# An attention and MoE kernel on one core: loads, splits, turns and swaps moved to other slots, stores a slot later, three buffers for turned k and q, one k turned on TensorE

## The chip, the cores and the metric

The kernel runs on one core of a Trainium2 chip. The metric is the time of one execution on the device in microseconds. Three runs of the kernel before gave 509.38, 513.93 and 518.40 us; the time before is their median, 513.93 us. A profile of one further execution is given below.

A core has a matrix engine (TensorE, PE in the profile; its weight loads are PEld), a vector engine (VectorE, DVE), a scalar engine (ScalarE, ACT), a general engine (GpSimd, POOL), and a sync engine (SyncE, SP). SP and ACT also issue DMA transfers, each from its own instruction queue (SPq and ACTq). An engine takes its instructions in program order.

## The reference

q, k and v are 8 batches of 8 heads, 576 rows of 64 numbers, in float32. The attention drops scores that are more than `tau` under their row's maximum; its output goes through two matrix products with `h - tanh(h)` between them.

```python
scores = scale * np.matmul(q, k.transpose(0, 1, 3, 2))
thresh = np.max(scores, axis=-1, keepdims=True) - tau
scores = np.where(scores >= thresh, scores, -1000000000.0)
scores = scores - np.max(scores, axis=-1, keepdims=True)
attn = np.exp(scores)
attn = attn / (np.sum(attn, axis=-1, keepdims=True) + 1e-09)
attn_out = np.matmul(attn, v)
# heads side by side: x is 4608 x 512
h = x @ w_in                      # 512 x 2048
out = (h - np.tanh(h)) @ w_out    # 2048 x 512
```

## The kernel before

**Tiles and slots.** Two heads make a pair, and there are 32 pairs, four to a batch. A pair has nine tiles of 128 score rows (`TPP = 9`), 288 tiles in all. The main loop (from L820) runs over slots, one tile to a slot: in slot `s` the scores of tile `s + 8` are computed (`AHEAD = 8`), the thresholded exponent of tile `s + 5` is begun (`kink`, L425, writes z), and tile `s` is weighted with v (`weights`, L442, and `attend`, L474). Between these the loop drops steps of the two MoE products of the batch four pairs back: `hidden` (L561, one step is four matmuls) and `project` (L589, likewise), in a pattern of 36 slots. After the 288 slots the MoE work that is left over runs alone.

**q and k.** The scores need q and k with more than half precision, so each is split into a high and a low float16 part. Each pair goes through a chain: load, split, turn, swap.

- Load: pairs 0 to 7 by SP (`load`, L174). From pair 8 on (`DUAL = 8`) by ACT's queue (`load_part`, L143), in five transfers: one for k, two for q, two for v. They fill `raw` buffers, two for each of k, q and v.
- Split: `split` (L222), three POOL instructions that write `khl` or `qhl` (two buffers each); `split_v` (L255), three POOL instructions.
- Turn: `turn` (L297) brings the head dimension onto the partitions. Up to pair 7 TensorE transposes nine 128x128 chunks into PSUM (L281) and DVE copies the result out (L313). From pair 8 on one DMA transpose issued by SP does it (L301). The results `kT` and `qT` are in a pool of two buffers.
- Swap: `swap` (L318), two POOL copies of 64x1152 (L323), which exchange the halves of kT into `kS`, also two buffers. Scores are the sum of q against kT and q against kS.

**z.** From pair 6 on, z of two tiles at a time is transposed by a DMA transpose issued by SP (L440) into `zT`; ACT takes the exponent of that (L469) as pT, the weights of `attend`. In pairs 0 to 5 TensorE does this transpose (L452, L461).

**What sets the order.** Nothing is scheduled automatically. For the chain of each pair there is a table of distances: an entry `("kt", 7)` in `LATER` puts the turn of k seven slots before the slot in which the pair's first scores are computed. Pairs 8 and up use one table for even and one for odd pairs; pairs 1 to 7 use `PREP` (L733) with exceptions. All steps of a slot's plan come at its end. In the tables k0 is the load of k, q0 and q1, v0 and v1 the two parts of the others, ks, qs and vs the splits, kt and qt the turns, kw the swap. SP's queue thus holds, in the order of the slots: the z transposes (in even slots), the turns of k and q, the output stores (L606), and in the beginning loads of q, k, v and the MoE weights. A store is collected in `stores` by `project` and issued in the next slot with the exception of the last one collected (L852 to L854), which waits for a later one.

Of the kernel before, what the change touches and what calls it, by code (L numbers as in the profile page):

```python
# [9 lines left out]
F32 = mybir.dt.float32  # L10
# [8 lines left out]
def kernel(  # L19
# [12 lines left out]
    P = 128  # L32

    B, H, S, D = q.shape
# [11 lines left out]
    HPAIR = H // 2  # L46
# [5 lines left out]
    TPP = 9  # L52
# [10 lines left out]
    AHEAD = 8  # L63
# [35 lines left out]
    for i in range(6):  # L99
# [8 lines left out]
    pool = lambda name, bufs, **kw: ctx.enter_context(  # L108
        tc.tile_pool(name=name, bufs=bufs, **kw)
    )  # L110
    PSUM = bass.MemoryType.PSUM
    raw_pool = pool("raw", 2)
    hl_pool = pool("hl", 2)
    qk_pool = pool("qk", 2)
    sc_pool = pool("sc", AHEAD - MASK + 2)
    st_pool = pool("st", 12)
    z_pool = pool("z", 4)
# [16 lines left out]
    raws = {}  # L134
    DUAL = 8
    AT_ONCE = 1
    LOADER = nc.scalar

    boths = {}

    def load_part(p, t, part):  # L143


        b, h0 = p // HPAIR, 2 * (p % HPAIR)
        if part == 0:
            both = raw_pool.tile([P, 2, 10, D], F32, name=f"{t}raw", tag=t)
            both = boths[t] = both[:, 0:AT_ONCE, :, :]
            for a in range(AT_ONCE):  # L150
                raws[p + a, t] = both[:, a, :, :]
        both = boths[t]
        rows = {"k": k, "q": q, "v": v}[t][b, h0 : h0 + 2 * AT_ONCE, :, :]
        heads = both.rearrange("p a (h c) d -> p (a h) (c d)", h=2)
        if t == "k":
            dst = both[:, :, 0:TPP, :].rearrange("p a c d -> p a (c d)")
            rows = rows.rearrange("(a h) s d -> a (h s) d", h=2).rearrange(
                "a (p c) d -> p a (c d)", c=TPP
            )
        elif t == "v":  # L160
            rows = rows.rearrange("h (p c) d -> p h (c d)", c=TPP)
            if part == 0:
                dst, rows = heads[0:64, :, 0 : 4 * D], rows[:, :, 0 : 4 * D]
            else:
                dst, rows = heads[64:P, :, :], rows[:, :, 4 * D :]
        elif part == 0:
            dst = heads[:, :, 0 : 4 * D]
            rows = rows[:, 0:512, :].rearrange("h (p c) d -> p h (c d)", c=4)
        else:
            dst = both[:, part - 1, 4, :]  # L170
            rows = rows[2 * part - 2 : 2 * part, 512:S, :].rearrange("h s d -> s h d")
        LOADER.dma_start(out=dst, in_=rows)

    def load(p, t):  # L174
        b, h0 = p // HPAIR, 2 * (p % HPAIR)
        hs = slice(h0, h0 + 2)
        src = {"k": k, "q": q, "v": v}[t]
        eng = nc.sync
        r = raw_pool.tile([P, 2, 10, D], F32, name=f"{t}raw", tag=t)[:, 0, :, :]
        raws[p, t] = r  # L180
        eng.dma_start(
            out=r.rearrange("p (h c) d -> p h (c d)", h=2)[:, :, 0 : 4 * D],
            in_=src[b, hs, 0:512, :].rearrange("h (p c) d -> p h (c d)", c=4),
        )
        rem = src[b, hs, 512:S, :].rearrange("h s d -> s h d")
        if t == "v":
            eng.dma_start(out=r[0:64, 4:10:5, :], in_=rem)
        else:
            eng.dma_start(out=r[:, 4, :], in_=rem)

    def load_first(t, h, eng):

        src = {"k": k, "q": q}[t]
        if (0, t) not in raws:
            raws[0, t] = raw_pool.tile([P, 2, 10, D], F32, name=f"{t}raw", tag=t)[:, 0, :, :]
        r = raws[0, t]
        if h is None:
            rem = src[0, 0:2, 512:S, :].rearrange("h s d -> s h d")
            eng.dma_start(out=r[:, 4, :], in_=rem)
        else:  # L200
            eng.dma_start(
                out=r[:, 5 * h : 5 * h + 4, :].rearrange("p c d -> p (c d)"),
                in_=src[0, h, 0:512, :].rearrange("(p c) d -> p (c d)", c=4),
            )
# [17 lines left out]
    def split(p, t):  # L222
        x = raws.pop((p, t))[:, 0:9, :]
        hl = hl_pool.tile([P, TPP, 2, D], FP16, name=f"{t}hl", tag=t)
        nc.gpsimd.tensor_scalar(  # L225
            out=x, in0=x, scalar1=QKSC, scalar2=1.0, op0=ALU.mult, op1=ALU.mult
        )
        nc.gpsimd.tensor_copy(out=hl[:, :, 0, :], in_=x)
        nc.gpsimd.tensor_tensor(  # L229
            out=hl[:, :, 1, :], in0=x, in1=hl[:, :, 0, :], op=ALU.subtract  # L230
        )
        hls[p, t] = hl
# [22 lines left out]
    def split_v(p):  # L255
        r, vb = raws.pop((p, "v")), vbs[p % NV]
        lo = 64 if p >= DUAL else 0
        nc.gpsimd.tensor_copy(
            out=vb[:, :, 0:4, 0:D],
            in_=r.rearrange("p (h c) d -> p h c d", h=2)[:, :, 0:4, :],  # L260
        )
        nc.gpsimd.tensor_copy(out=vb[0:64, :, 4, 0:D], in_=r[lo : lo + 64, 4:10:5, :])
        nc.gpsimd.tensor_copy(out=vb[64:P, :, 5, 0:D], in_=r[lo : lo + 64, 4:10:5, :])
# [13 lines left out]
    def turn_chunk(out, c, lhsT, mixed=True):  # L277
# [4 lines left out]
            out=out, lhsT=lhsT, rhs=rhs, is_transpose=True, start=True, stop=True  # L282
        )

    def k_lead(p):
        if p < HPAIR + 2:
            return 6 if p in (2, 4) or p == HPAIR + 1 else 5 - (p == 1)
        return (6, 6)[1 - p % 2]

    def q_by_dma(p):  # L290

        return p >= DUAL

    def k_by_dma(p):
        return p >= DUAL

    def turn(p, t):  # L297
        hl = hls.pop((p, t))
# [260 lines left out]
    gs, stores = {}, []  # L559
# [159 lines left out]
    def w_load(piece):  # L719
# [6 lines left out]
        else:  # L726
# [18 lines left out]

    LATER = {
        0: (
            ("k0", 17), ("q0", 15), ("v0", 13), ("kt", 7), ("q1", 15),
            ("ks", 8), ("v1", 12), ("vs", 6), ("qs", 10), ("qt", 7),
            ("kw", 3),  # L750
        ),
        1: (
            ("k0", 19), ("v1", 14), ("q0", 18), ("v0", 16), ("qs", 11),
            ("q1", 17), ("qt", 8), ("ks", 13), ("vs", 6), ("kt", 10),
            ("kw", 7),
        ),
    }
    for p in range(DUAL, NPAIR):
        first = TPP * p - AHEAD
        at = lambda d, f: plan.setdefault(first - d, []).append(f)  # L760
        for what, d in LATER[p % 2]:
            t, w = what
            f = {
                "0": lambda p=p, t=t: load_part(p, t, 0),
                "1": lambda p=p, t=t: load_part(p, t, 1),
                "2": lambda p=p, t=t: load_part(p, t, 2),
                "s": lambda p=p, t=t: split_v(p) if t == "v" else split(p, t),
                "t": lambda p=p, t=t: turn(p, t),
                "w": lambda p=p, t=t: swap(p) if k_by_dma(p) else None,
            }[w]  # L770
            at(d, f)
    for p in range(1, DUAL):
        first = TPP * p - AHEAD
        for d, f in PREP[3 if p == 1 else 0 :]:
            d -= p == 1 and d == 3
            if p > HPAIR and d >= LDK - 2:
                d = ((16, 14, 12), (17, 15, 13))[1 - p % 2][LDK - d]
            elif d in (7, 8) and q_by_dma(p):
                d = ((9, 9) if d == 7 else (10, 10))[1 - p % 2]
            elif d == 4:  # L780
                d = 4
            elif d == 5:
                d = k_lead(p)
            elif p in (2, 4):
                d = {8: 9, 7: 8}.get(d, d)
            plan.setdefault(first - d, []).append(lambda p=p, f=f: f(p))
        d = (6, 7)[1 - p % 2] if q_by_dma(p) else 3 - (p == 1 or p >= 5)
        d = 4 if p in (2, 4) else d
        plan.setdefault(first - d, []).append(lambda p=p: turn(p, "q"))

    load(0, "v")
# [8 lines left out]
        load(1, t)  # L800
    pieces = w_pieces()
    load_when = [3, 8, 13, 18, 21, 25, 29, 34, 38, 42, 46, 49, 52, 55, 58, 61]
    cast_when = [11, 19, 27] + [4 * i + 32 for i in range(3)] + [3 * i + 44 for i in range(10)]

    todo, stage = [], 0
    fold = const.tile([P, 64], BF16, name="fold")

    for at in sorted(plan):
# [1 line left out]
            plan.setdefault(-AHEAD, []).extend(plan.pop(at))  # L810


    kinks, wts, atts = {}, {}, {}
    for i in range(NTILE + 3):
        at = i - 4 if i < HPAIR * TPP else i
        atts.setdefault(at + LAG, []).append(i)
        if i < NTILE:
            wts.setdefault(at, []).append(i)
            kinks.setdefault(i // 2 * 2 + 2 - AHEAD if i < 4 else i - MASK, []).append(i)
    for s in range(-AHEAD, NTILE + LAG + 3):  # L820
        p, j = divmod(max(s, 0), TPP)
# [27 lines left out]
                out=fold, in0=ident_bf[:, 0:64], in1=ident_bf[:, 64:P], op=ALU.add  # L849
            )  # L850
        shrink()
        for store in stores[:-1]:  # L852
            store()
        del stores[:-1]  # L854
        for i in atts.pop(s, []):
            pp, jj = divmod(i, TPP)
# [8 lines left out]
                emit_x(pp - 1)  # L865
        for step in plan.pop(s, []):
            step()
        if s + AHEAD in cast_when:
            w_cast()
        if s + AHEAD in load_when:  # L870
            w_load(next(pieces))

    for _, step in todo:
        step()
        bend()
        shrink()
        for store in stores:
            store()
        stores.clear()
# [10 lines left out]
    _ = bass_utils  # L890
# [35 lines left out]
```

## Time and profile before

| what | value |
|---|---|
| median of three runs | 513.93 us (509.38 to 518.40) |
| the profiled execution's own time | 509.47 us |
| its span | 507.7 us |
| PE, ACT, DVE, POOL busy | 484.1, 432.7, 400.0, 291.1 us |
| mean granted TensorE clock | 0.995 |
| DMA queue q1 (issued by SP) | 213520 packets, 73.17 MB, 74.7% of 16 engines' span |
| DMA queue q10 (issued by ACT) | 20944 packets, 21.67 MB, 15.7% |
| DMA transposes issued by SP | 117 of z, 24 of k, 24 of q |

The profile is of one execution; its span begins with the first instruction and ends with the last, and 1.8 us of the time lie around it. A group's busy time is the union of its instructions; "idle before" is how long the engine stood still just before them and what ended that. Idle time of an engine with spare time costs nothing. Matmuls overlap each other, so that the mean duration of one is longer than its share of the busy time: 256 matmuls of 512 columns with a mean of 381 ns each have 97.4 us together.

### The profile page before, as it was taken

The numbers are of one execution on the slowest core, as the hardware profiler recorded it, in microseconds if no ns is written. First come the engines' busy times: TensorE is split into PE (matmuls) and PEld (weight loads), VectorE is DVE, ScalarE is ACT, GpSimd is POOL, SyncE is SP. The second block draws the span as 40 slices with busy tenths as digits, with TensorE's granted clock in tenths as the row PEclk, the third lists the DMA queues.
The fourth block names the chain that finished last, engine by engine and source line by source line (L and its number), as shares of the span: only waits on it lengthen the run. The fifth ranks groups of instructions, "written<-read, shape, count | busy, mean of one in ns | idle before, by whom it ended". The sixth has DMA issues, their size and how long they took to land.

```text
span 507.7 us, 12146 instructions
## 1 busy us (share of the span) xinstructions
PE 484.1 (95%) x4274; PEld 270.4 (53%) x4336; DVE 400.0 (79%) x1149; ACT 432.7 (85%) x617; POOL 291.1 (57%) x390
## 2 busy tenths in 40 slices
PE   8999899888999999999999999999998999999997
PEld 4667566444555555555555555555554555544444
DVE  5899979976989898988898889889887887544440
ACT  5999999988999999999999999999998999533430
POOL 7999999967676657574757575575567500000000
PEclk9999999998999999999999999999999999999999
DMA  6852658999999999999999999999999976211013
GB/s 198 264 163 90 196 176 220 226 189 220 211 245 228 242 227 223 242 249 211 228 228 268 216 228 228 223 231 231 212 220 252 197 131 113 76 41 43 24 40 83
DMA packets 234525, 95.61 MB, mean 188 GB/s; under 512 B 205152, under 2 KB 223840, under 8 KB 234464
## 3 DMA queue, kind: packets, MB, share of 16 engines
q1 hardware_dynamic: 213520, 73.17, 74.7%
q10 hardware_dynamic: 20944, 21.67, 15.7%
q8 instruction: 34, 0.56, 0.5%
q14 instruction: 27, 0.22, 0.1%
HBM read 36.70 MB, written 9.44 MB: 91 GB/s over the span
## 4 chain that ended last, share of the span: by engine, by line
PE 61%; POOL 12%; DMA 10%; ACT 6%; issue 5%; DVE 3%; ACTq 1%; SPq 0%; POOLq 0%
PE psY L591 20%; PE psH L565 16%; PE psS L396 14%; PE psO L499 4%; DMA zT<-z 3%; POOL kS L323 3%; PE psHt L565 3%; ACT pT L469 3%; ACT z L433 2%; DMA kT<-khl 2%; DMA kraw<-in_k_dram 2%; PE psS L387 2%; ACT th L578 1%; POOL w_in_sb L717 1%; DMA qraw<-in_q_dram 1%
## 5 line engine op out<-in xcount | busy, mean ns | idle before, releaser
L406 DVE TENSOR_SCALAR_CACHE_REDUCE sc<-psS 128x576 f32<-128x576 f32 x288 | 213.2, 752 | 28.7 <-PE psS L396 14.2
L433 ACT ACTIVATE z<-sc,nb 128x576 bf16<-128x576 f32 x288 | 217.2, 770 | 13.5 <-DVE nb L418 9.4
L591 PE MATMUL psY<-w_out_sb,g 128*128 128x512 bf16 (+1 forms) x564 | 141.5, 375 | 1.7 <-DVE nb L418 0.2
L469 ACT ACTIVATE pT<-zT 128x1152 f16<-128x1152 bf16 x117 | 135.0, 1154 | 4.6 <-DMA zT<-z 4.6
L565 PE MATMUL psH<-xT,w_in_sb 128*128 128x512 bf16 x448 | 118.8, 379 | 5.3 <-DVE g L584 2.2
L323 POOL COPY kS<-kT 64x1152 f16<-64x1152 f16 x62 | 70.7, 1141 | 74.6 <-DMA kT<-khl 55.2
L584 DVE SCALAR_TENSOR_TENSOR g<-th,psH 128x512 bf16<-128x512 f32 x128 | 87.6, 684 | 28.9 <-ACT th L578 28.1
L396 PE MATMUL psS<-kT,qT 128*128 128x512 f16 (+1 forms) x512 | 104.8, 286 | 3.3 <-DVE sc L406 1.5
L396 PE MATMUL psS<-kS,qT 128*128 128x512 f16 (+1 forms) x512 | 104.9, 287 | 0.1
L396 PEld LDWEIGHTS <-qT 128*128 128x128 f16 x1024 | 72.8, 98 | 58.6 <-issue 4.2
L578 ACT ACTIVATE th<-psH 128x512 f32<-128x512 f32 x128 | 74.6, 583 | 20.9 <-PE psH L565 20.9
L591 PEld LDWEIGHTS <-g 128*128 128x128 bf16 x592 | 51.3, 98 | 55.1 <-issue 1.1
L565 PEld LDWEIGHTS <-w_in_sb 128*128 128x128 bf16 x576 | 49.0, 98 | 57.3 <-issue 5.5
L499 PE MATMUL psO<-vb,pT 128*128 128x65 bf16 x1024 | 53.6, 195 | 0.0
L499 PEld LDWEIGHTS <-pT 128*128 128x128 f16 x1024 | 44.5, 98 | 9.9
L229 POOL TENSOR_TENSOR qhl<-qraw,qhl 128x576 f16<-128x576 f32 x31 | 39.7, 1281 | 2.6
L229 POOL TENSOR_TENSOR khl<-kraw,khl 128x576 f16<-128x576 f32 x31 | 39.7, 1280 | 2.6
L461 ACT ACTIVATE pT<-psZ 128x512 f16<-128x512 bf16 (+1 forms) x54 | 35.1, 653 | 2.5 <-PE psZ L452 2.3
L225 POOL TENSOR_SCALAR qraw<-qraw 128x576 f32<-128x576 f32 x31 | 20.8, 670 | 20.9 <-DMA qraw<-in_q_dram 19.6
L603 DVE COPY yo<-psY 128x512 f32<-128x512 f32 (+1 forms) x31 | 21.1, 680 | 13.3 <-PE psY L591 12.4
L492 PE MATMUL psO<-vb,pT 128*128 128x130 bf16 x128 | 28.3, 221 | 2.1 <-ACT pT L469 1.8
L525 DVE TENSOR_TENSOR osb<-psO,rc 128x256 bf16<-128x256 f32 x64 | 27.2, 425 | 2.2
(77 smaller groups left out, 448.6 us busy)
## 6 DMA issues: line engine op xcount, KB each, us to landing
out_dram<-yo SPq DMA_DIRECT2D x32, 256.0 KB, 2.9
kraw<-in_k_dram ACTq DMA_DIRECT2D x24, 288.0 KB, 4.2
qraw<-in_q_dram ACTq DMA_DIRECT2D x24, 256.0 KB, 4.1
wt<-in_moe_w_in_dram SPq DMA_DIRECT2D x8, 512.0 KB, 4.6
wt<-in_moe_w_out_dram SPq DMA_DIRECT2D x8, 512.0 KB, 4.2
vraw<-in_v_dram ACTq DMA_DIRECT2D x24, 160.0 KB, 4.0
vraw<-in_v_dram ACTq DMA_DIRECT2D x24, 128.0 KB, 4.2
vraw<-in_v_dram SPq DMA_DIRECT2D x8, 256.0 KB, 3.6
```

The lines of the kernel that those rows point to most:

```text
L229: nc.gpsimd.tensor_tensor(out=hl[:, :, 1, :], in0=x, in1=hl[:, :, 0, :], op=ALU.subtract)
L323: nc.gpsimd.tensor_copy(out=o, in_=i)
L396: nc.tensor.matmul(out=ps[:, dst], lhsT=lhs, rhs=cols(p, kk, hh), start=(n == 0), stop=(n == 1),)
L406: nc.vector.tensor_scalar(out=sc, in0=ps[:, lo : lo + S], scalar1=SC, scalar2=None, op0=ALU.mult, op1=ALU.max, accum_out=mx[:, c : c + 1],)
L433: nc.scalar.activation(out=z, in_=sc, func=ACT.Prelu, bias=nb, scale=1.0, alpha=STEEP)
L461: nc.scalar.activation(out=pt[:, off * P : (off + n) * P], in_=ps[:, 0 : n * P], func=ACT.Exp)
L469: nc.scalar.activation(out=pt[:, 0 : n * P], in_=zts.pop(i)[:, 0:n, :], func=ACT.Exp)
L499: nc.tensor.matmul(out=po[:, t - 1 + ab, :], lhsT=pt[:, blk * P : (blk + 1) * P], rhs=vb[:, hh, c, :], start=False, stop=(n == 7), skip_gr ...
L565: nc.tensor.matmul(out=ps, lhsT=w_in_sb[:, c, n * P : (n + 1) * P], rhs=xs[m][:, c, :] if m < B else xR[:, c, :, :], start=(c == 0), stop= ...
L578: nc.scalar.activation(out=th, in_=ps, func=ACT.Tanh)
L584: nc.vector.scalar_tensor_tensor(out=gs[m][:, n, :], in0=th, scalar=-1.0, in1=ps, op0=ALU.mult, op1=ALU.add,)
L591: nc.tensor.matmul(out=ps, lhsT=gs[m][:, n, ms * P : (ms + 1) * P], rhs=w_out_sb[:, n, cols], start=(n == 0), stop=(n == DF_C - 1),)
```

## The change

The instructions are the same but for pair 8's turn of k, and their order on ACT's queue, POOL and SP is changed. On TensorE and DVE only two places move: the turn of k of pair 5 comes one slot later, and the turn of k of pair 8 is added.

- New tables of distances for the even and odd pairs from 10 on, and own ones (`FIRST_LATER`) for pairs 8 and 9.
- `qk_pool` has three buffers instead of two for each of kT, qT and kS. The raw tiles lose a half that was not used.
- `k_by_dma` holds from pair 9 on, so pair 8's k is turned by TensorE and DVE, as in pairs 1 to 7, and its swap is issued by POOL directly after that.
- A store is issued one slot later than before (`going`).
- `LEADS` writes the distances of pairs 1 to 7 as a table; the only value that differs is pair 5's turn of k, 5 in place of 6. `V_PARTS`, `SOONER`, the list `cast_when` and the `count` loops express what was there before.

```diff
-    qk_pool = pool("qk", 2)
+    qk_pool = pool("qk", 3)
...
-            both = raw_pool.tile([P, 2, 10, D], F32, name=f"{t}raw", tag=t)
-            both = boths[t] = both[:, 0:AT_ONCE, :, :]
+            both = raw_pool.tile([P, AT_ONCE, 10, D], F32, name=f"{t}raw", tag=t)
+            boths[t] = both
...
+    LEADS = {
+        1: (8, 7, 4, 4, 2),
+        2: (9, 8, 6, 4, 4),
+        3: (8, 7, 5, 4, 3),
+        4: (9, 8, 6, 4, 4),
+        5: (8, 7, 5, 4, 2),
+        6: (8, 7, 6, 4, 2),
+        7: (8, 7, 6, 4, 2),
+    }
...
     def k_by_dma(p):
-        return p >= DUAL
+        return p > DUAL
...
     LATER = {
         0: (
-            ("k0", 17), ("q0", 15), ("v0", 13), ("kt", 7), ("q1", 15),
-            ("ks", 8), ("v1", 12), ("vs", 6), ("qs", 10), ("qt", 7),
-            ("kw", 3),
+            ("kt", 11), ("qt", 7), ("k0", 18), ("q0", 17), ("v0", 13),
+            ("q1", 14), ("v1", 10), ("ks", 12), ("qs", 8), ("vs", 4),
+            ("kw", 6),
+        ),
+        1: (
+            ("kt", 10), ("qt", 6), ("k0", 18), ("q0", 14), ("v0", 15),
+            ("q1", 13), ("v1", 12), ("ks", 11), ("qs", 8), ("vs", 6),
+            ("kw", 5),
+        ),
+    }
+    FIRST_LATER = {
+        8: (
+            ("k0", 18), ("q0", 15), ("v0", 14), ("kt", 7), ("q1", 15),
+            ("ks", 8), ("v1", 12), ("vs", 6), ("qs", 10), ("qt", 5),
+            ("kw", 3),
         ),
-        1: (
-            ("k0", 19), ("v1", 14), ("q0", 18), ("v0", 16), ("qs", 11),
-            ("q1", 17), ("qt", 8), ("ks", 13), ("vs", 6), ("kt", 10),
-            ("kw", 7),
+        9: (
+            ("kt", 10), ("qt", 6), ("k0", 18), ("q0", 14), ("v0", 15),
+            ("q1", 13), ("v1", 12), ("ks", 11), ("qs", 8), ("vs", 6),
+            ("kw", 5),
         ),
     }
...
-        for what, d in LATER[p % 2]:
+        for what, d in FIRST_LATER.get(p) or LATER[p % 2]:
...
-        for store in stores[:-1]:
+        for store in going:
             store()
+        going = stores[:-1]
         del stores[:-1]
...
+    for store in going:
+        store()
     for _, step in todo:
```

More of the change, by code (lines that the diff above doesn't have):

```diff
@@ L136 @@
     AT_ONCE = 1
+    V_PARTS = ((0, 0, 4), (64, 4, 9))
     LOADER = nc.scalar
@@ L161, in load_part @@
             rows = rows.rearrange("h (p c) d -> p h (c d)", c=TPP)
[L162 to L165, printed above, removed]
+            at, c0, c1 = V_PARTS[part]
+            dst = heads[at : at + 64, :, c0 % 4 * D : (c1 - c0 + c0 % 4) * D]
+            if c0 == 8:
+                dst = heads[at : at + 64, :, 4 * D : 5 * D]
+            rows = rows[:, :, c0 * D : c1 * D]
         elif part == 0:
@@ L178, in load @@
         eng = nc.sync
-        r = raw_pool.tile([P, 2, 10, D], F32, name=f"{t}raw", tag=t)[:, 0, :, :]
+        r = raw_pool.tile([P, AT_ONCE, 10, D], F32, name=f"{t}raw", tag=t)[:, 0, :, :]
         raws[p, t] = r
@@ L194, in load_first @@
         if (0, t) not in raws:
-            raws[0, t] = raw_pool.tile([P, 2, 10, D], F32, name=f"{t}raw", tag=t)[:, 0, :, :]
+            raws[0, t] = raw_pool.tile([P, AT_ONCE, 10, D], F32, name=f"{t}raw", tag=t)[:, 0, :, :]
         r = raws[0, t]
@@ L779 @@
                 d = ((9, 9) if d == 7 else (10, 10))[1 - p % 2]
+            elif p in LEADS and d in (8, 7, 5, 4):
+                d = LEADS[p][(8, 7, 5, 4).index(d)]
             elif d == 4:
@@ L787 @@
         d = (6, 7)[1 - p % 2] if q_by_dma(p) else 3 - (p == 1 or p >= 5)
-        d = 4 if p in (2, 4) else d
+        d = LEADS[p][4] if p in LEADS else d
         plan.setdefault(first - d, []).append(lambda p=p: turn(p, "q"))
@@ L802 @@
     load_when = [3, 8, 13, 18, 21, 25, 29, 34, 38, 42, 46, 49, 52, 55, 58, 61]
-    cast_when = [11, 19, 27] + [4 * i + 32 for i in range(3)] + [3 * i + 44 for i in range(10)]
+    cast_when = [11, 19, 27, 32, 36, 40, 44, 47, 50, 53, 56, 59, 62, 65, 68, 71]
     todo, stage = [], 0
+    going = []
     fold = const.tile([P, 64], BF16, name="fold")
@@ L810 @@
             plan.setdefault(-AHEAD, []).extend(plan.pop(at))
+    SOONER = (4, 4, 4, 4, 0, 0, 0)
     kinks, wts, atts = {}, {}, {}
     for i in range(NTILE + 3):
-        at = i - 4 if i < HPAIR * TPP else i
+        at = i - SOONER[min(i // TPP, 6)]
         atts.setdefault(at + LAG, []).append(i)
@@ L867 @@
             step()
-        if s + AHEAD in cast_when:
+        for _ in range(cast_when.count(s + AHEAD)):
             w_cast()
-        if s + AHEAD in load_when:
+        for _ in range(load_when.count(s + AHEAD)):
             w_load(next(pieces))
+    for store in going:
+        store()
     for _, step in todo:
```

## The prediction

> **What bounds the kernel now.** First the slices of the page: who is full, and at which clock.
>
> ```profile
> PE   8999899888999999999999999999998999999997
> ...
> ACT  5999999988999999999999999999998999533430
> POOL 7999999967676657574757575575567500000000
> PEclk9999999998999999999999999999999999999999
> DMA  6852658999999999999999999999999976211013
> ```
>
> PE is full but for slices 8 to 10 and 31; ACT is nearly as full until slice 34. Up to slice 8 POOL is full too. The clock dips once, in slice 10. The DMA engines are full from slice 7 to 32, where z, k and q are turned by DMA.
>
> Second, busy time by stretch. From 102.4 us on I cut where a batch of four pairs begins (read off the score evictions, L406: 36 tiles, 36 evictions).
>
> ```profile
> core 0: us, PE busy (x) PEld busy (x) DVE busy (x) ACT busy (x) POOL busy (x), PEclk, DMA share, GB/s
> 62.00:102.40 40.40, 37.14 (x401) 23.43 (x405) 34.09 (x101) 37.25 (x59) 37.57 (x46) 1.00 0.88 212
> 102.40:158.80 56.40, 52.02 (x452) 28.45 (x460) 46.66 (x139) 53.01 (x73) 37.53 (x48) 0.97 1.18 215
> 158.80:211.70 52.90, 52.27 (x466) 28.75 (x473) 46.92 (x139) 51.46 (x72) 34.93 (x45) 1.00 1.18 233
> ...
> 264.60:317.40 52.80, 52.17 (x465) 28.73 (x472) 46.81 (x138) 51.40 (x71) 33.86 (x44) 1.00 1.17 231
> 317.40:371.40 54.00, 52.62 (x465) 28.88 (x472) 46.87 (x139) 51.57 (x72) 34.18 (x44) 1.00 1.21 227
> 371.40:426.60 55.20, 53.06 (x456) 28.73 (x463) 45.48 (x134) 50.41 (x70) 22.09 (x28) 1.00 0.99 181
> ```
>
> The batches from 158.8 to 317.4 (the one left out reads like its neighbours) take 52.9 us with PE busy for 52.3: nothing that is moved on POOL, SP or ACT's queue can make these shorter. What a better order can win lies in the other three: 56.4 - 52.9 = 3.5 us, 54.0 - 52.9 = 1.1, and 55.2 - 52.6 = 2.6 (the last batch should end 0.3 earlier, since its last pair took 12.7 where that place has 13.0). Together 7.2 us. After 426.6 PE runs the MoE remainder at 76.9 of 81.1 us, untouched.
>
> Third, the chain of waits inside these three, and the clock beside the first:
>
> ```profile
> 99.62 3.73 DMA zT<-z
> 109.77 5.31 DMA zT<-z
> 307.03 5.84 DMA kT<-khl
> 324.27 6.96 DMA zT<-z
> 374.98 6.59 DMA qraw<-in_q_dram
> ```
>
> ```profile
> 114.00:117.00 3.00, 1.32 (x17) 1.00 1.19 249
> 117.00:120.00 3.00, 2.39 (x15) 0.56 0.94 267
> 120.00:123.00 3.00, 3.00 (x27) 0.87 1.79 178
> ```
>
> In the steady batches the chain is matmuls alone; here it leaves PE for a transfer that lands late. ACT then waits for zT, and PE for ACT's pT. The clock's part in the first is 3 x 0.44 + 3 x 0.13 = 1.7 us, the other 1.8 are waits.
>
> **Why the transfers are late.** The page has 213520 packets on q1 in 74.7% of 507.7 us: 0.747 x 507.7 x 16 / 213520 = 28 ns each. If a transpose of 128x1152 is 1152 packets (165 of them would be 190,080), one takes 1152 x 28 / 16 = 2.0 us of all engines, by this estimate; a pair issues 4.5 of z and 2 of k and q, 13.2 us of DMA in a pair's 13.2 us. DMA has no slack, and what arrives bunched queues. Before, the turns stand at slots -7 and -7 (even pair), -1 and +1 (odd pair, nine slots on) in a period of 18: two in one slot, then a hole of ten.
>
> **The change part by part.**
>
> *New distances, pairs 10 to 31.* Turns go to -11, -7, -1 and +3: gaps of 4, 6, 4, 4 and never two in a slot. From turn of k to swap it is 5 slots, not 4 or 3; a slot is 13.2 / 9 = 1.47 us, so 7.3 us against 5.9 or 4.4, and kT landed up to 5.8 us after its issue. The waits this is about:
>
> ```profile
> POOL kS L323 <- DMA kT<-khl: 55.2, 18, 4.7
> POOL qraw L225 <- DMA qraw<-in_q_dram: 19.6, 9, 3.5
> POOL kS L323 <- PE psH L565: 9.2, 2, 4.8
> SPq L301 <- POOL qhl L229: 8.8, 8, 1.3
> ```
>
> Of the 55 us nearly all is POOL's own slack (it is busy 34 of 52.9 us), worth nothing; only where the late swap pushes the next split and turn, as at 307 to 324 us, did PE pay. Loads keep 5 to 7 slots before their split (q1 of even pairs 6 for 5, odd 5 for 6; v1 of odd pairs 6 for 8), so the kind of wait at 374.98 is spread out, not excluded. Of the 1.1 + 2.6 = 3.7 us I take 3.4 back.
>
> *Three qk buffers.* An even turn of k at -11 comes before the scores of the pair two earlier are done (-9); with two buffers SP would stand there, with z behind it. The waits of a swap on PE (9.2 us above) go too. Cover: POOL slack, so 0 by themselves; without the third buffer two slots, 2.9 us, in every other pair.
>
> *Pair 8's k on TensorE.* Removes one DMA transpose (2.0 us of DMA) and 2.6 us of SP at 93 us, just ahead of the first stall. Adds nine PE transposes: 72 of them are busy 5.5 us, 76 ns each, 0.7 us on PE; one DVE copy (0.76 us, L313), and one PSUM buffer of the scores for that time. POOL stands behind them: its split of this k ended at 92.8, and the swap follows at once, about 2 us of waiting with weight casts, v and pair 9's split behind it. Before, POOL waited 4.3 us at 106 to 110, so it has that to give. A rule of the Trainium skill speaks against this part: "TensorE: Matmul & The Clock Gate", Part 4, has about 275 ns for such a transpose in a kernel, and a DVE copy after it. That would be 2.5 us, 1.8 more; the row here overlaps them, and I use the row.
>
> Late next: qT of pair 8 goes from 7 slots ahead to 5. PE already waited 0.7 us for it at the start of pair 8 (101 us), beside 1.0 us for kS. The kS wait goes, qT's stays or grows to 1 us; I count nothing won there. Of the batch's 3.5 us I take 2.6: the 1.7 of the clock, and 1.6 of waits, less the 0.7 on PE.
>
> The clock is the second place where a rule weighs in. The same page, Part 1, says that the clock drops after an idle window of about 3.4 us. PE's longest gap here is 1.8 us (ended by pT at 117.4), busy 1.32 of 3 us, and the clock fell to 0.56 all the same. By the rule this gap did not cause the drop and its 1.7 us stay; by the row they go with the stall. I side with the row; by the rule my sum is 1.7 worse.
>
> *Stores a slot later.* In the loop SP waited for a store's source for 7.2 us in 18 short waits (L606 <- DVE), with at most 0.6 us at once, and zT behind it came in time. The issue (0.55 us) is the same, one z transpose later. Value 0; the cover is zT's lead. The buffer (two yo) is refilled every nine slots on average, so it is no new wait.
>
> *Pair 5's turn of k a slot later.* PE waited for khl three times, 1.0 us in all. Between +0.3 and -0.5 us; 0, as ACT (37.25 of 40.4) and POOL pace that stretch.
>
> *A new wait.* Splits stood 3 or 1 slots before their turn; now 1, only odd q has 2. A split lasts 0.67 + 0.66 + 1.28 = 2.6 us, a slot 1.47, so SP stands about 1.2 us for POOL at 34 of 47 turns, with the next z transpose behind. No row shows it in this number; the nearest is SPq L301 <- POOL above (1.3 us at most, and there the z behind it came in time). The turns are in odd slots and z in even ones, so the delay of z is the wait plus the issue (1.3) less a slot, at most 1. By the trace a zT landed 2.07 us before its exponent began in the mean, 0.39 in the tenth percentile. Bounds: 0 where the lead holds, and 0.4 x 47 = 19 us if each turn uses it up by 0.4 us more than it has. I take 0, since with the turns spread a transpose should land sooner by as much.
>
> **Sum.** 3.4 + 2.6 = 6.0 us: span 507.7 - 6.0 = 501.7, and with the 1.8 around it 503.5. That is against the profiled execution (509.47), which lies 4.5 under the median of the runs. I read the spread of those runs, 509.4 to 518.4, as the same late transfers in other places, which go too; were it kept, the median would be near 508.
>
> **Rivals.**
>
> 1. *The lateness moves.* DMA work per pair is unchanged (one transpose of 165 gone), the share stays 1.18, and z transposes land at other wrong moments. For it: no slack in DMA by the estimate. Against: three batches in this state lost nothing. Half of the 7.2 is lost elsewhere: 505 to 513 us.
> 2. *SP waits for POOL.* Slower. Mechanism and price above: a turn queued one slot behind its split, z behind the turn. It decides once the mean loss passes 0.35 us a turn: 47 x 0.35 = 16.4, less the 6.0 gained, is the 10.3 us that make 2%. At 0.35 to 0.5 us a turn the time is 520 to 531. For it: a tenth of the z transposes have under 0.39 us to give. Against: 2.07 us in the mean.
> 3. *More than the sum.* The stretch 62 to 102.4, with PE idle for 3.3 us, gains too when POOL's swap of pair 8 comes forward, and the q wait doesn't appear: 496 to 500.
>
> That the change does nothing is no case: SP's and POOL's orders differ at every pair from 8 on.
>
> **How the numbers follow.** 2% of 513.93 is 10.3 us, about what a measurement of this kernel can tell from no change: faster is below 503.7. The forecast has 0.64, between 499 and 508, two thirds of it under the mark as it stands (0.42). Rival 3 has 0.10, rival 1 0.17, rival 2 0.09 (with 0.02 of it under 2%, offset by as much of rival 1 above). Faster 0.42 + 0.10 = 0.52, same 0.22 + 0.17 = 0.39, slower 0.09. The likeliest case gives 503.5. From 498 to 512 holds the forecast, most of rival 1 and half of rival 3.
>
> **What would show it.** Right: batches from 102 us to the end at 52.9 us each; clock 1.00 in slice 10; POOL's wait for kT near nothing; no k, q load or kT on the chain. The new wait: SPq L301 <- POOL rises from about 20 us (100 to 426 us) to 40 or more in sum; harmless if ACT pT <- DMA zT stays below the 4.6 us of before. Wrong: batches still over 54 us with zT in the chain (rival 1), ACT waiting for zT by more than 10 us in sum (rival 2), or a steady batch that is no longer 52.9.

## The result and the profile after

| | before | changed |
|---|---|---|
| median of 20 runs | 513.71 us | 508.90 us |
| lowest and highest | 509.38 and 518.91 | 503.36 and 517.11 |
| ratio to before, 95% interval | 1 | 0.9897 (0.9869 to 0.9925) |

The change makes the kernel about 1% faster, 5.3 us (3.9 to 6.7) of 513.7; the medians are 4.8 us apart. That is clear of zero, and within the 2% that the prediction took as the bound. The time lies inside the range of 498 to 512; the point forecast was 503.5. The ratios here and below leave out executions more than 1.5% above the fastest of their kernel (seven of the changed kernel's 20, the profiled one among them), while the medians are of all runs.

The profiled execution of the changed kernel took 511.62 us (span 509.7), more than its median, as the profiled execution of before (509.47) was one of the quickest of its kind. So the two spans must not be subtracted; the profiles show where time goes, and the ratios how much. The slices of the page:

```profile
PE   8999899889999989999999999999998999999997
...
ACT  5999998889999889999999999899979999533430
...
PEclk9999999989999999999999999999999999999999
DMA  7852658999999999999999999999999986311013
```

DMA is as full as before, and the clock still dips once, now in slice 8. The same stretches as in the prediction, cut at the starts of this execution's batches (columns: stretch, its length, then busy time and number of instructions of PE, PEld, DVE, ACT and POOL, then granted clock, DMA share, GB/s):

```profile
62.00:105.00 43.00, 37.11 (x406) 23.63 (x412) 34.67 (x102) 38.88 (x61) 38.86 (x48) 0.99 0.90 196
105.00:158.00 53.00, 51.83 (x452) 28.38 (x460) 46.39 (x138) 50.97 (x71) 36.11 (x46) 0.97 1.15 225
158.00:212.50 54.50, 52.63 (x466) 28.73 (x473) 46.51 (x139) 51.41 (x72) 33.75 (x45) 1.00 1.21 216
212.50:265.40 52.90, 52.27 (x466) 28.75 (x473) 46.89 (x139) 51.38 (x72) 37.02 (x48) 1.00 1.19 243
...
372.60:428.60 56.00, 53.08 (x456) 28.80 (x463) 45.66 (x134) 50.34 (x70) 21.53 (x28) 1.00 1.02 177
```

The batch of pairs 8 to 11 takes 53.0 us, not 56.4; but 2.6 us have gone into the stretch ahead of it (pairs 6 and 7), and the second batch, which lost nothing before, takes 54.5. The losses stand in other places than in the profile of before. Who waited (waiting group, what ended the wait: total us, times, longest):

```profile
POOL kS L337 <- DMA kT<-khl: 72.7, 20, 7.9
...
POOL qraw L228 <- DMA qraw<-in_q_dram: 10.8, 7, 2.8
ACT pT L483 <- DMA zT<-z: 10.6, 11, 2.2
...
PEld L410 <- DMA qT<-qhl: 1.7, 1, 1.7
PE psS L410 <- DMA qT<-qhl: 1.6, 1, 1.6
```

And the longest transfers in the chain of waits (start, duration), all of z:

```profile
91.28 9.46 DMA zT<-z
...
167.12 14.69 DMA zT<-z x2
...
280.47 5.17 DMA zT<-z
```

Loads of v stand in the chain at 100.77 and 368.07 us and one of q at 258.60, for 2.6 to 4.7 us. The chain leaves PE in the same manner as before: for a transpose of z that lands late. The wait for pair 8's qT, which the prediction named as what is late next, is the 1.6 us of the last line of waits.

### The profile page after: what moved, and what is told of

It is laid out like the page before. It is cut to its first block, busy times and chain, and to the rows that moved or that the text cites. A ratio compares the mean times of both kernels' runs of the same rounds, so it can differ in the third digit from the quotient of the medians.

```text
span 509.7 us, 12184 instructions
## 1 busy us (share of the span) xinstructions
PE 484.8 (95%) x4283; PEld 270.9 (53%) x4345; DVE 400.2 (79%) x1150; ACT 431.7 (85%) x617; POOL 291.4 (57%) x390
## 3 DMA queue, kind: packets, MB, share of 16 engines
q1 hardware_dynamic: 212336, 72.87, 75.1%
## 4 chain that ended last, share of the span: by engine, by line
PE 57%; POOL 12%; DMA 9%; issue 7%; ACT 7%; DVE 5%; ACTq 1%; SPq 0%; POOLq 0%; DVEq 0%
PE psY L605 18%; PE psH L579 14%; PE psS L410 13%; DMA zT<-z 6%; PE psO L513 3%; POOL kS L337 3%; PE psHt L579 3%; ACT pT L483 3%; DMA vraw<-in_v_dram 3%; ACT z L447 2%; DVE g L598 2%; POOL qhl L232 2%; DVE sc L420 2%; PE psS L401 2%; ACTq L175 1%
## 5 line engine op out<-in xcount | busy, mean ns | idle before, releaser
L483 ACT ACTIVATE pT<-zT 128x1152 f16<-128x1152 bf16 x117 | 135.2, 1155 | 12.3 <-DMA zT<-z 10.6
L337 POOL COPY kS<-kT 64x1152 f16<-64x1152 f16 x62 | 70.8, 1142 | 86.3 <-DMA kT<-khl 72.7
L410 PE MATMUL psS<-kS,qT 128*128 128x512 f16 (+1 forms) x512 | 105.1, 287 | 0.0
L605 PEld LDWEIGHTS <-g 128*128 128x128 bf16 x592 | 51.1, 98 | 54.6 <-DVE g L598 0.4
```

The lines of the kernel that those rows point to most:

```text
L337: nc.gpsimd.tensor_copy(out=o, in_=i)
L410: nc.tensor.matmul(out=ps[:, dst], lhsT=lhs, rhs=cols(p, kk, hh), start=(n == 0), stop=(n == 1),)
L483: nc.scalar.activation(out=pt[:, 0 : n * P], in_=zts.pop(i)[:, 0:n, :], func=ACT.Exp)
L605: nc.tensor.matmul(out=ps, lhsT=gs[m][:, n, ms * P : (ms + 1) * P], rhs=w_out_sb[:, n, cols], start=(n == 0), stop=(n == DF_C - 1),)
```

## The experiments

**The parts of the change alone.** Four kernels, each against the kernel before.

The new distances from pair 10 on, with three buffers; pairs 1 to 9 and the stores as before. Against the changed kernel:

```diff
-        return p > DUAL
+        return p >= DUAL
...
     FIRST_LATER = {
         8: (
-            ("k0", 18), ("q0", 15), ("v0", 14), ("kt", 7), ("q1", 15),
-            ("ks", 8), ("v1", 12), ("vs", 6), ("qs", 10), ("qt", 5),
+            ("k0", 17), ("q0", 15), ("v0", 13), ("kt", 7), ("q1", 15),
+            ("ks", 8), ("v1", 12), ("vs", 6), ("qs", 10), ("qt", 7),
...
         9: (
-            ("kt", 10), ("qt", 6), ("k0", 18), ("q0", 14), ("v0", 15),
+            ("k0", 19), ("v1", 14), ("q0", 18), ("v0", 16), ("qs", 11),
...
```

> The kernel before with the new distances of pairs 10 to 31 and three buffers for kT, qT and kS; pairs 1 to 9, the turn of pair 8's k and the stores as before. Theory of the prediction: these distances are worth 3.4 of the 6.0 us, ratio to before about 0.993, and batches from 158.8 us on at 52.9 us. Rival (the gain is made at pairs 8 and 9 alone): ratio 1.00, late batches still at 54 to 55 us.

Measured: 0.9922 (0.9895 to 0.9948), 509.66 us in the median. The distances are worth 4.0 us (2.7 to 5.4), by themselves most of the gain.

The new distances of pairs 8 and 9, pair 8's k on TensorE, and three buffers; from pair 10 on, and the stores, as before. Against the changed kernel:

```diff
     LATER = {
         0: (
-            ("kt", 11), ("qt", 7), ("k0", 18), ("q0", 17), ("v0", 13),
-            ("q1", 14), ("v1", 10), ("ks", 12), ("qs", 8), ("vs", 4),
-            ("kw", 6),
+            ("k0", 17), ("q0", 15), ("v0", 13), ("kt", 7), ("q1", 15),
+            ("ks", 8), ("v1", 12), ("vs", 6), ("qs", 10), ("qt", 7),
+            ("kw", 3),
...
```

> The kernel before with three buffers, the new distances of pairs 8 and 9, pair 8's k turned on TensorE and pair 5's turn of k a slot later; pairs 10 to 31 and the stores as before. Theory of the prediction: 2.6 us, ratio about 0.995, clock without a dip, the batch of pairs 8 to 11 near 54 us. Rival (the late qT of pair 8 takes back what the missing transpose gives): ratio 0.999 to 1.00, PE waiting 1 us or more for qT at the start of pair 8.

Measured: 0.9971 (0.9940 to 1.0001). That is 1.5 us (0 to 3.1), between the two expectations. The two parts multiply to 0.9893, the whole change.

Three buffers and nothing else, `pool("qk", 3)` in the kernel before:

> The kernel before with three buffers for kT, qT and kS and nothing else. Theory of the prediction: a swap's waits for PE go, but POOL has slack, ratio 1.00. Rival (the two buffers held SP with z transposes behind it): ratio about 0.995 and SP without waits of turns for PE.

Measured: 0.9984 (0.9952 to 1.0017), no difference that shows.

The stores where they were:

```diff
-        for store in going:
+        for store in stores[:-1]:
             store()
-        going = stores[:-1]
         del stores[:-1]
```

> The changed kernel with the stores issued where they were before. Theory of the prediction: the stores are worth nothing, ratio to before about 0.990 as for the whole change. Rival (the store's issue and wait ahead of a z transpose costs): ratio about 0.993 or above.

Measured: 0.9874 (0.9826 to 0.9923). It overlaps the 0.9897 of the whole change, so no gain from moving the stores shows. The six runs lie at 503.57 to 508.28 us, all under the changed kernel's median of 508.90; whether the move costs something stays open.

**Pair 8's k, and its q.**

```diff
     def k_by_dma(p):
-        return p > DUAL
+        return p >= DUAL
```

> The changed kernel with pair 8's k turned by DMA (seven slots ahead, swap three slots ahead), all else as changed. Theory of the prediction: the transpose taken off DMA and SP at the first stall is most of the 2.6 us of the head, ratio to before 0.993 to 0.995. Rival: TensorE's turn costs what it saves, 0.987 to 0.990 as with the change.

Measured: 0.9985 (0.9955 to 1.0015), 511.52 us. The intervals of this and of the whole change lie apart, with 4.5 us between the two ratios; between the medians (511.52 and 508.90) there are 2.6 us. So half of the gain or more is gone without TensorE's turn of one k. Its profile between 88 and 120 us, POOL's row and the waits:

```profile
99.43 2.33 POOL L337 COPY kS<-kT 64x1152 f16<-64x1152 f16 x2 [3.36 <-DMA kT<-khl]
...
101.85 0.67 POOL L228 TENSOR_SCALAR kraw<-kraw 128x576 f32<-128x576 f32 x1
```

```profile
PE psS L410 <- DMA qT<-qhl: 3.4, 1, 3.4
POOL kS L337 <- DMA kT<-khl: 3.4, 1, 3.4
```

In the new order the swap of pair 8 stands ahead of pair 9's split on POOL, and q's turn two slots later than before on SP. With kT from DMA, POOL waits 3.36 us and the split of pair 9 with it, and PE stands 3.4 us for a qT that was issued behind the kT. The stall is not this execution's alone, it seems: the granted clock, which drops where PE stands long enough (last section), was at 0.997 or lower in 17 of the 22 runs of this kernel and in 4 of the 20 of the changed one.

How long the head takes can be read in every profile, from the first score eviction of pair 4 to that of pair 12. Here are this kernel (DMA turn, new order), the first one above (DMA turn, old order), and the head alone (TensorE's turn, new order):

```profile
51.10:158.40 107.30, 98.78 (x965) 57.74 (x978) 90.66 (x269) 99.54 (x146) 85.16 (x106) 0.97 0.99 212
```

```profile
51.10:158.40 107.30, 98.86 (x984) 57.50 (x982) 90.35 (x270) 99.39 (x145) 84.43 (x106) 1.00 1.02 210
```

```profile
51.10:155.60 104.50, 98.13 (x990) 57.71 (x987) 91.22 (x271) 99.62 (x146) 84.45 (x106) 1.00 1.00 213
```

The kernel before takes 107.5 us, the one with the buffers alone 107.7. The four other kernels with TensorE's turn that keep the changed kernel's loads and its lead for z (one above, three below) take 103.9 to 105.1; only the changed kernel's own profiled execution, with its stall at 91 us, takes 107.0. So TensorE's turn is worth about 3 us in the head, and the DMA turn costs as much in the old order as in the new one. What it is that the turn cures was not separated. It can be the order of POOL and SP just described, or the load on DMA: the kernel before without v loads from pair 10 on (below) keeps the old order and the DMA turn, and takes 104.2. TensorE's turn with the old tables of pairs 8 and 9 was not run.

```diff
-            ("ks", 8), ("v1", 12), ("vs", 6), ("qs", 10), ("qt", 5),
+            ("ks", 8), ("v1", 12), ("vs", 6), ("qs", 10), ("qt", 7),
```

> The changed kernel with pair 8's q turned seven slots ahead, as before the change, instead of five. Theory: PE's wait for this qT (1.7 us in the changed kernel's profile) goes, and half of it comes back in time: ratio to before 0.988. Rival: the z transposes take the place of qT in the queue and are late instead, 0.990 as with the whole change.

Measured: 0.9867 (0.9825 to 0.9909). PE's wait for qT is not in its profile any more, but no gain in the time shows: the median is 508.47 us, against 508.90 for the whole change. This run, the next two and the one with loads added are set against runs of the kernel before with a median of 515.08 us, so their ratios come out a little lower than the others.

**What keeps the rest.** Three theories were left: z has too little lead; POOL's waits for kT hold up the queues; the DMA engines are full.

More lead for z:

```diff
-    MASK = 5
+    MASK = 6
...
-    sc_pool = pool("sc", AHEAD - MASK + 2)
+    sc_pool = pool("sc", 5)
```

The second edit keeps the five buffers for the scores that there were before.

> The changed kernel with z begun six slots ahead of its tile instead of five, so each z transpose may be issued a slot (1.47 us) sooner; nothing else differs. Theory: what still costs time in both kernels is z transposes that land just after ACT wants them (in the changed kernel's profile a zT landed 1.67 us before its exponent in the mean, a tenth of them 0.08 or less, ACT waiting 10.6 us for zT); the lead then rises by about 1.4 us, ACT's wait for zT falls under 3 us, ratio to before 0.98 or less. Rival: the DMA engines deliver no sooner, they are full, and ACT now waits for DVE's nb: ratio 0.99 or above.

Measured: 1.0313 (1.0282 to 1.0345), slower. The first half of the theory holds: zT now lands 4.57 us before its exponent in the mean, and no wait of ACT for zT is left among the waits. But ACT now asks for the maximum of two tiles (nb, made by DVE) one slot after the scores of the second:

```profile
ACT z L447 <- DVE nb L432: 35.7, 76, 1.6
```

Its batches, cut at their first score evictions, from pairs 4 to 7 on (one is left out):

```profile
51.00:110.70 59.70, 48.20 (x529) 30.18 (x527) 45.61 (x134) 48.16 (x76) 47.94 (x59) 1.00 0.69 180
...
166.70:222.60 55.90, 53.98 (x475) 29.18 (x474) 46.50 (x140) 52.04 (x71) 34.15 (x44) 1.00 1.20 219
222.60:278.60 56.00, 54.05 (x475) 29.36 (x474) 46.53 (x140) 52.13 (x71) 37.21 (x48) 1.00 1.08 226
```

A batch takes 56.0 us in place of 52.9, with PE standing for 1.9 of them, and pairs 4 to 7 take 59.7 where the kernel before has 51.1. That the wait for nb is the cause of all of it is not shown. The slot that z gained was taken from the time between scores and maximum, so this run can't tell what the lead alone would be worth.

POOL's waits:

```diff
     LATER = {
         0: (
...
-            ("kw", 6),
+            ("kw", 1),
...
         1: (
...
-            ("kw", 5),
+            ("kw", 2),
```

> The changed kernel with the swap of pairs 9 to 31 placed behind the next pair's split of k on POOL (one and two slots ahead of its first use in place of six and five). Theory: POOL standing at a swap for kT (72.7 us in 20 waits in the changed kernel's profile) holds back the next split, its turn on SP and the z transposes behind that; now POOL's wait for kT falls below 15 us, SP's wait for POOL at the turns from 39 us to under 20, ratio 0.985. Rival: POOL's waits are its own slack, ratio 0.990 as for the whole change; or PE waits for kS at the start of a pair and it is slower.

Measured: 0.9866 (0.9832 to 0.9900), overlapping the 0.9897 of the whole change; the medians are 508.17 and 508.90 us. In its profile:

```profile
POOL kraw L228 <- DMA kraw<-in_k_dram: 30.8, 21, 4.0
...
POOL qraw L228 <- DMA qraw<-in_q_dram: 28.6, 11, 4.2
...
POOL kS L337 <- DMA kT<-khl: 4.1, 5, 1.0
```

Of the 72.7 us 4.1 are left and POOL waits for loads instead; SP's waits for POOL at the turns fell only from 39 to 37 us over the span. The waits at the swap were slack.

The DMA engines: one load more per pair from pair 10 on (`extra` loads k again, 288 KB, into a tile that nobody reads), and the v loads less.

```diff
+        if p >= 10:
+            at(16, lambda p=p: extra(p))
```

> The changed kernel with one more load for each of the pairs 10 to 31: k once more, 288 KB, issued by ACT into a tile that nobody reads. Theory: DMA has no slack; a k load takes about 1.0 us of all 16 engines (its 2304-byte packets between 158.8 and 317.4 us of the first profile), 22 of them 22 us, and at least half of that shows: ratio to before 1.01 or above. Rival: DMA is not full, lateness comes from the order alone: ratio 0.990 to 0.993.

```diff
-        r, vb = raws.pop((p, "v")), vbs[p % NV]
+        r, vb = raws.pop((p, "v")) if p < 10 else v8[:, 0, :, :], vbs[p % NV]
...
+        if t == "v" and p >= 10:
+            return
```

> The changed kernel without the v loads of pairs 10 to 31: their v is split from pair 8's, which stays in a tile of its own (so the output is that of another v). 22 x 288 KB are taken off the DMA engines, as much as the extra k loads added. Theory: DMA has no slack and that is where the late transposes come from; the batches from 158.8 us on fall to 52.9 us, ratio to before 0.975 to 0.98. Rival: in the changed kernel the order has already taken out what can be had, ratio 0.99.

> The kernel before with the same v loads left out, so the output is that of another v. Theory: the change gains only because DMA is full, by evening out what queues; with room in DMA the old order comes to the same pace, ratio to before 0.975 to 0.983 and within 0.4% of the changed kernel without these loads. Rival: the new order is better by itself (POOL and SP stand less): the distance of about 1% between the two stays, ratio 0.985 to 0.99.

| kernel | ratio to before | median us (lowest to highest) |
|---|---|---|
| changed, 22 loads more | 1.0340 (1.0300 to 1.0380) | 532.08 (530.56 to 547.97) |
| changed | 0.9897 (0.9869 to 0.9925) | 508.90 (503.36 to 517.11) |
| changed, no v loads from pair 10 on | 0.9815 (0.9774 to 0.9857) | 502.92 (502.71 to 503.61) |
| before | 1 | 513.71 (509.38 to 518.91) |
| before, no v loads from pair 10 on | 0.9832 (0.9786 to 0.9877) | 503.55 (502.90 to 506.27) |

Each ratio is against runs of the kernel before in the same session (medians 515.08 us for the first row, 513.75 for those without v loads). 22 loads, 22 us of DMA by the estimate, cost 22.8 us (0.0443 of 513.7), about as much. Part of that is the clock, which fell in the stalls: it was granted at 0.983 to 0.996 in all seven runs, and 0.987 is up to 6.9 us of 532. With as much taken off, both orders run at the same speed, 0.2% apart with intervals that overlap, and the spread of the runs falls from 14 us (changed) and 10 (before), over 20 runs, to 1 and 3 over 6. With room in DMA the new order has nothing left to win. The two profiles without v loads, the changed kernel and then the one before:

```profile
158.80:211.70 52.90, 52.27 (x466) 28.77 (x473) 46.86 (x139) 51.50 (x71) 34.67 (x44) 1.00 1.10 212
211.70:264.60 52.90, 52.27 (x466) 28.75 (x472) 46.88 (x139) 51.49 (x71) 34.66 (x44) 1.00 1.06 206
```

```profile
158.80:211.70 52.90, 52.27 (x466) 28.77 (x473) 46.91 (x138) 51.37 (x71) 34.51 (x44) 1.00 1.16 209
211.70:264.60 52.90, 52.27 (x466) 28.77 (x473) 46.90 (x139) 51.50 (x71) 33.61 (x44) 1.00 1.06 211
```

52.27 of 52.90 us of PE is the pace that PE sets. With the loads added, ACT's wait for zT in the profile (of an execution of 547.97 us, the slowest of that kernel) is

```profile
ACT pT L489 <- DMA zT<-z: 35.9, 16, 5.0
```

against 10.6 us in the changed kernel and none in the one without v loads. These edits also change what ACT's queue issues: 22 issues more (10.2 us together), 44 of about 0.6 us fewer. By the traces that costs ACT nothing, since an issue runs while ACT computes. Of the 58.7 us of its issues after 100 us in the changed kernel's profile, and of the 10.2 us added, none falls into a time in which ACT stood idle. So it is the load on DMA, and ACT's wait for zT follows it in all three.

**Three edits at once.** Stores where they were, q of pair 8 seven slots ahead, and the late swaps:

> The changed kernel with three edits at once: stores where they were before, pair 8's q turned seven slots ahead, swaps behind the next split of k. Theory: each removes some waiting of POOL, SP or PE ahead of z transposes, ratio to before 0.983 or less. Rival: DMA is full and none of these changes its load, so it stays where each of them was alone, 0.987 to 0.990.

Measured: 0.9882 (0.9819 to 0.9945), 507.80 us in the median, in the same place as each alone. No version was found that is clearly faster than the changed kernel.

## Why the prediction was right or wrong

**Where there was something to win: right, but for the last batch.** 52.9 us a batch was read as PE's pace, out of reach of any order. Both kernels without v loads run at it, and take 502.9 and 503.6 us. The forecast of 503.5 is the time with nothing lost, not the time of the change. The last batch was to take 52.6 us, though its own row has PE busy for 53.06; the two kernels without v loads take 53.5 for it, so 1.7 us could be won there, not 2.6.

**The sizes of the parts: right within their intervals.** Distances 3.4 forecast, 4.0 (2.7 to 5.4) measured; the head 2.6 forecast, 1.5 (0 to 3.1) measured; buffers and stores 0, and no difference measured. The sum of 6.0 stands against 5.3 (3.9 to 6.7). Inside the head the shares were wrong: 1.7 us were put down to the clock. But of 97 runs of the kernel before with their clock on record only 19 fell to 0.997 or lower, and the two kernels with the old head and no dip (the new distances, the buffers alone) still took 107.3 and 107.7 us for it. So the waits alone can make up the 3 us. Which of the new distances wins the 4.0 was not separated.

**The step that failed** is the last of the sum: "I read the spread of those runs, 509.4 to 518.4, as the same late transfers in other places, which go too". The first half holds: with room in DMA the spread goes. The second doesn't: DMA's load is unchanged, so lateness and spread stay (503.36 to 517.11). The longest batch is another from profile to profile. Apart from the last one, it is pairs 12 to 15 in the changed kernel's (54.5 us), pairs 24 to 27 with late swaps (56.0), and pairs 20 to 23 with three edits at once (58.2). The prediction gave its own alternative, "were it kept, the median would be near 508", and measured were 508.9. Its own argument, 13.2 us of DMA in a pair's 13.2 us, spoke against the step; so did the profile's time, 4.2 us below the median: an execution so near the best shows less lateness than is usual, and a gain counted in it may not be set against its own time as if the usual lateness were none. In effect rival 1, to which it gave 0.17, is what came: half of the loss went, the rest moved; and its sign, batches over 54 us with zT in the chain, is in the profile after. "Faster" by over 2% needed the failed step; "same" at 0.39 came.

**DMA has no slack: right**, by an estimate that left something out. One transpose less took 1184 packets from q1 (213520 to 212336), so the 1152 assumed were near. But 13.2 us of DMA in 13.2 us leave out ACT's loads: 15.7% of 507.7 us are another 3.3 us for each of 24 pairs. With them the sum passes the time that there is, as the DMA share of 1.18 does, so the times of packets overlap, and 28 ns is more than one costs its engine. That DMA is full is shown by the loads added and taken away.

**Pair 8's k: sign and size right, the reason open.** It was to relieve DMA and SP. Its head is 3 us shorter, as told above, and 2.6 were forecast; the order of POOL and SP, which may not bear that kT at this place, is a rival that was not ruled out. The cost of the PE transposes by the row was right: 81 of them are busy 6.2 us in the changed kernel, 77 ns each. The mean duration of one is 219 ns, so they overlap, and the skill's 275 ns, for one transpose, are not what each of nine costs. (The 256 matmuls of 512 columns that were given as an example of overlap with the profile of before do not overlap: 256 times 381 ns are the 97.4 us that they have together.) POOL's wait for the swap was 1.9 us, and about 2 were expected. The qT that was called late next was late, by 1.6 us.

**POOL's wait for kT near nothing: wrong.** It rose from 55 to 73 us. More slots between turn and swap are not the reason: with the old distances it is 76.0 us (head alone) and 82.5 (buffers alone). The two kernels without v loads have 52.1 and 54.5, so the load on DMA has a part in it; the rest of the cause stays open. As valued, it cost nothing: the late swaps removed it, and the time stayed.

**The new wait of SP: right in amount** (38 us between 100 and 426 us, against 21), and it did no harm that was seen: the kernels with the old distances show ACT waiting for zT as much (13.7 us with the head alone, 15.8 with the buffers alone). Rival 2 did not come. The test by ACT's wait for zT was not a good one. The kernel before has 4.6 us in an execution of 509.47 us, and with the buffers alone, which change nothing in the time, it has 15.8 in one of 516.97. It tells executions apart, not kernels.

**The clock: the row was right, the rule too narrow.** See below.

## What to carry to other kernels

Before counting a gain in a profile, see where that execution stands among the runs: losses that come and go are smallest in the quickest one, and its time is not the base for a usual run. Where a resource is full, a better order takes out part of the waiting and leaves its load and its spread; adding and removing a known amount of that load tells in two runs whether it is full. Look at the granted clock of many runs before a dip in one profile is counted as a loss: here one run in five had it.

## What the runs showed of the hardware that was not expected

The TensorE clock fell to half for a stretch of 3.4 us after a stretch of the same length in which PE had been busy for less than some 40%, with no gap in it over 1.81 us. Stretches of before, of the changed kernel, and of the changed kernel with q of pair 8 at seven slots:

```profile
114.00:117.40 3.40, 1.33 (x18) 1.00 1.18 267
117.40:120.80 3.40, 3.18 (x17) 0.50 0.97 240
```

```profile
100.90:104.30 3.40, 1.08 (x14) 1.00 1.23 268
104.30:107.70 3.40, 3.18 (x15) 0.50 1.49 242
```

```profile
174.20:177.60 3.40, 1.42 (x16) 1.00 1.10 245
177.60:181.00 3.40, 3.22 (x25) 1.00 1.17 216
```

1.33 and 1.08 us of work brought the clock down, 1.42 us did not, though the third has the longest gap of these (2.05 us). The clock's stretches in a profile begin at whole multiples of 3.413 us from each other. Counted on that grid, the 14 profiles have 2069 stretches at full clock. The 20 of them in which PE was busy for 1.39 us or less were followed by half clock, and none of the others, all with 1.45 or more, was. Back at full clock it was after half-clock stretches with 3.0 us of work and more; two with 2.46 and 2.58 us were followed by another at half. The Trainium skill ("TensorE: Matmul & The Clock Gate", Part 1) has the window of about 3.4 us, which these runs show, and a drop after an idle one; here the window was not idle. The price is at most 1.7 us for each such stretch, half of it.
